# Two loads and a split moved: the first expert's second weights behind the last query and key loads, and the tail of the value split behind the second transposes, in an attention, expert and feed-forward kernel

## The chip, the cores and the metric

The kernel runs on one core of one Trainium2 chip. The metric is the device time of one execution in microseconds (us). A time without another source is that of the profiled execution of the kernel before.

## What is computed

Three layers follow one another: sigmoid attention over 4 batches of 12 heads (448 tokens, head size 64), a layer of 8 experts in which each of the 1792 tokens goes to the one with its highest logit, and a dense feed-forward layer.

```python
attn = 1.0 / (1.0 + np.exp(-(scale * q @ k.T - np.log(S))))
x = (attn @ v)                      # per head, then [1792, 768]
expert_idx = np.argmax(x @ w_gate, axis=1)
for e in range(8):                  # tokens of expert e
    h = np.maximum(xe @ w1[e], 0.0) # 768 -> 1024
    out[mask] = gate_w[mask, None] * (h @ w2[e])   # 1024 -> 768
h = x @ w_in                        # 768 -> 2048
out = (h / (1.0 + np.exp(-h))) @ w_out
```

## The kernel before, in words

Every fp32 matrix that TensorE multiplies is split into a high part (a rounded copy, fp32r) and a low part (the remainder), and a product is made of three matmuls: high by high, high by low, low by high. A split is therefore a cast and a subtraction. For weights ScalarE (ACT) does the casts (`w1h`, `w2h`) and VectorE (DVE) the subtractions (`w1l`, `w2l`); the last of the eight `w2l` of an expert is done by GpSimd (POOL).

**Attention.** The heads come in 24 pairs. `load` (lines 170 to 179) requests a pair's query `qf`, key `kf` and value `vf` on SyncE's (SP's) queue three pairs ahead. The loop at line 618 goes through two groups of keys at a time: `scores`, then `av` of the groups before; in between DVE splits the next pair's key (`split_k`) and query (`split_q`). The program's order is written out by hand, each engine works its own list in order, and so does SP with its requests. SP's requests share eight completion semaphores in turn: a request whose semaphore is still held by an unfinished transfer waits, with all requests behind it.

**The first expert.** When three of the four batches are routed, `choose` (line 360) finds the expert with most tokens and requests its weights: `w1` in six transfers of 512 KB into `stage1` (line 383) and `w2` in eight of 384 KB into `stage2` (line 385). After them stand the requests for the last pair. During the last groups `wsplit0` (line 604) splits `w1`.

**The expert tiles.** The tokens, sorted by expert, are worked in tiles of 128 rows (loop at line 791), 21 at the most. In a tile: `l1` (lines 693 to 698) gives the hidden layer in two halves; `relu`; `htrans` (line 705) transposes a half on TensorE (line 708), ACT casts it from PSUM (`hh`, line 711) and DVE subtracts (`hl`, line 712); `l2` (lines 715 to 723) takes the eight slices `w2h`/`w2l`, slices 0 to 3 with the first half and 4 to 7 with the second. In between `xtrans` transposes the next tile's rows, and `prep(t + 2)` computes which rows tile t + 2 takes: on DVE `jk` (line 531), a `SCALAR_TENSOR_TENSOR` with two inputs in SBUF, and `gi` (line 534), then on POOL the gather `gx` (line 537).

**Change of expert.** Where the tile's expert is another than the last tile's (`fr > 0`, known on ACT, DVE, SP and POOL), the new `w2` is split in two parts: slices 0 to 4 before the first `htrans` (line 807) and slices 5 to 7 (`SA` is 5) after `xtrans` (line 821). `w1` of a new expert is split at the end of the tile before (line 834): six casts and six subtractions. Each split is followed by the request for the next expert's weights into the staging tile just read. Seven tiles change the expert; they are called by their index here: 4, 5, 6, 10, 11, 13 and 16. In 4, 5 and 10 the tile after changes it as well, so that a split of `w1` ends them. The first halves' transposes of two successive tiles delimit a tile's period in what follows.

**The feed-forward layer** follows and streams its own weights.

Of the kernel before, what the change touches and what calls it, by code (L numbers as in the profile page):

```python
# [36 lines left out]
TMAX = (N + E * 127) // 128  # L37
# [20 lines left out]
def attn_moe_ffn(ctx: ExitStack, tc, qT, kT, v, wg, w1, w2, w_in, w_out, out):  # L58
    nc = tc.nc
# [67 lines left out]
    stage2 = RS.pool("stage2", 1).tile([128, FC, DM], F32, name="stage2")  # L127
# [70 lines left out]
    NG = 4  # L198
# [162 lines left out]
    def choose():  # L361
        yield 0
        pn = px_[1][:, 448:448 + E]
        nc.tensor.matmul(out=pn, lhsT=ones, rhs=run, start=True, stop=True)
        yield 0
        mx = rt.tile([128, 1], F32, tag="cmx", name="cmx")
        nc.vector.tensor_reduce(out=mx, in_=pn, axis=AX.X, op=ALU.max)
        yield 1
        cd = rt.tile([128, E], F32, tag="ccd", name="ccd")
        nc.vector.tensor_scalar(out=cd, in0=pn, scalar1=mx[:, 0:1], scalar2=-16.0, op0=ALU.is_ge, op1=ALU.mult)  # L370
        yield 1
        nc.vector.tensor_add(out=cd, in0=cd, in1=iota_e)
        yield 1
        nc.vector.tensor_reduce(out=mx, in_=cd, axis=AX.X, op=ALU.min)
        yield 1
        nc.vector.tensor_scalar(out=es, in0=mx, scalar1=16.0, scalar2=None, op0=ALU.add)
        yield 1
        nc.vector.tensor_copy(out=es_i, in_=es)
        nc.vector.tensor_scalar(out=pg_t[:, 0:1], in0=es, scalar1=float(PG), scalar2=None, op0=ALU.mult)
        yield 0  # L380
        er = reg(es_i[0:1, 0:1], (SP,), E - 1)
        for i in range(KC):
            nc.sync.dma_start(out=stage1[:, i], in_=w1[bass.ds(er, 1), :, i].rearrange("a p f -> (a p) f"))
        for f in range(FC):
            nc.sync.dma_start(out=stage2[:, f], in_=w2[bass.ds(er, 1), :, f].rearrange("a p f -> (a p) f"))
        yield 1

    def advance(x, n):
        while n > 0:
# [138 lines left out]
    def prep(t, nt=N):  # L528
        tk = keep(gs4, [128, 1], F32, "tk", t % 4)
        jk = keep(gs4, [128, NPG], F32, "jk", t % 4)  # L530
        nc.vector.scalar_tensor_tensor(out=jk, in0=iota_pg, scalar=pg_t[:, t:t + 1], in1=tt_all,
                                       op0=ALU.is_equal, op1=ALU.mult, accum_out=tk)
        gi = keep(gs4, [128, 1], I32, "gi", t % 4)
        nc.vector.tensor_scalar(out=gi, in0=tk, scalar1=-1.0, scalar2=0.0, op0=ALU.add, op1=ALU.max)
        off = bass.IndirectOffsetOnAxis(ap=gi, axis=0)
        gx = keep(gp, [128, DM], F32, "gx", t % 2)
        nc.gpsimd.indirect_dma_start(out=gx, out_offset=None, in_=Xd[0:nt], in_offset=off,
                                     bounds_check=nt - 1, oob_is_err=False)
        return gx, gi, tk
# [46 lines left out]
    def keep0():  # L586
        wi = xr_p[1].tile([128, 2, DM], F32R, tag="xr", name="wi0")
        nc.scalar.copy(out=wi[:, 0], in_=done[1])
        nc.vector.tensor_sub(out=wi[:, 1], in0=done[1], in1=wi[:, 0])
        wi0.append(wi)  # L590
# [4 lines left out]
    G = UG * len(units)  # L595
# [22 lines left out]
    for k in range(0, G + LAG, 2):  # L618
        if k < G:
            if k % NG == 0 and k // NG + 3 < G // NG:  # L620
                load(k // NG + 3)
            scores(k)
            scores(k + 1)
        xforms()
        if LAG <= k < G + LAG:
            av(k - LAG)
            av(k - LAG + 1)
        pn = k // NG + 1
        if pn < G // NG:
            if k % NG == 0:  # L630
                split_tiles(pn)
                split_k(pn)
            else:
                split_q(pn)
        if k >= LAG and (k - LAG) % NG == NG - 2:
            pr = (k - LAG) // NG
            evac(pr)
            xq += [(pr, 0), (pr, 1)]
        if k >= G - UG:
            wsplit0((k - G + UG) // 2)  # L640
        for j in (k, k + 1):
            background(j)
            if cur is None and j >= G - 8 and not tasks:
                cur = prep(0, (B - 1) * S)
                gg = gate(0, cur[1], (B - 1) * S)
            if j >= 4 * UG and j % 8 == 1 and TMIN + (j - 4 * UG) // 8 < TMAX:
                t = TMIN + (j - 4 * UG) // 8
                nc.sync.dma_start(out=Yd[t * 128:(t + 1) * 128], in_=zero)
# [56 lines left out]
    def htrans(t, half, hs):  # L705
        pt = px_[half]
        for j in range(HB // 128):
            nc.tensor.transpose(pt[:, j * 128:(j + 1) * 128], hs[:, j * 128:(j + 1) * 128], ident)
        hh = keep(hp, [128, HB], F32R, f"hh{half}", 0)
        hl = keep(hp, [128, HB], F32R, f"hl{half}", 0)  # L710
        nc.scalar.copy(out=hh, in_=pt)  # L711
        nc.vector.tensor_sub(out=hl, in0=pt, in1=hh)  # L712
        return hh, hl

    def l2(py, hh, hl, fs):
        for f in fs:
            c = slice((f % 4) * 128, (f % 4) * 128 + 128)
            for n in range(2):
                ys = slice(n * YB, n * YB + YB)
                o = py[:, n, 0:YB]  # L720
                nc.tensor.matmul(out=o, lhsT=hh[:, c], rhs=w2h[:, f, ys], start=(f == 0), stop=False)  # L721
                nc.tensor.matmul(out=o, lhsT=hh[:, c], rhs=w2l[:, f, ys], start=False, stop=False)  # L722
                nc.tensor.matmul(out=o, lhsT=hl[:, c], rhs=w2h[:, f, ys], start=False, stop=(f == FC - 1))  # L723
# [4 lines left out]
    def psy(t):  # L728
        return keep(ps_y, [128, 2, 512], F32, "y", 0)
# [24 lines left out]
    h0 = htrans(0, 0, hs0)  # L754
    hs1 = relu(0, 1, ph1)
    until(x3, "tt")
    split2(range(2, 4), (3,))
    nxt, nn = prep(1), prep(2)
    raws.append(rload(0))
    py = psy(0)  # L760
    l2(py, *h0, range(0, 2))
    h1 = htrans(0, 1, hs1)
# [31 lines left out]
    for t in range(TMAX):  # L794
        if t == TMIN - 1:
            xts = xload(0)
        if t >= TMIN:
            live = reg(tbl[0:1, 1, t:t + 1], (PE, ACT, DVE, SP, POOL), 1)
            ifs.enter_context(tc.If(live > 0))
        gx, gi, tk = cur  # L800
        if t > 0:
            gg = gate(t, gi)
            ph0, ph1 = psh(t, 0), psh(t, 1)
            l1(ph0, 0, *xhl, range(KC))
            l1(ph1, 1, *xhl, range(0, 3))
            if t > 1:
                with tc.If(fr > 0):
                    split2(range(0, SA))
                    if t + 1 < TMAX:
                        nc.sync.dma_start(out=stage2[:, 0:SA], in_=wsrc(w2, ne, 0, SA))  # L810
            if t == 3:
                early()
            h0 = htrans(t, 0, relu(t, 0, ph0))
            l1(ph1, 1, *xhl, range(3, KC))
            hs1 = relu(t, 1, ph1)
            if t + 1 < TMAX:
                xhl = xtrans(t + 1, nxt[0])
            if len(done) >= 2 and not wi0:
                keep0()
            if t > 1:  # L820
                with tc.If(fr > 0):
                    split2(range(SA, FC))
                    if t + 1 < TMAX:
                        nc.sync.dma_start(out=stage2[:, SA:], in_=wsrc(w2, ne, SA, FC))
            nn = prep(t + 2) if t + 2 < TMAX else None
            py = psy(t)
            l2(py, *h0, range(0, 2))
            h1 = htrans(t, 1, hs1)
            l2(py, *h0, range(2, 4))
            l2(py, *h1, range(4, 8))  # L830
        if 0 < t and t + 1 < TMAX:
            fr = reg(tbl[0:1, 0, t + 1:t + 2], (ACT, DVE, SP, POOL), 1)
            ne = reg(tbl[0:1, 2, t + 1:t + 2], (SP,), E - 1)
            with tc.If(fr > 0):
                for k in (0, KC // 2):
                    split1(range(k, k + KC // 2))
                    if t + 2 < TMAX:
                        nc.sync.dma_start(out=stage1[:, k:k + KC // 2], in_=wsrc(w1, ne, k, k + KC // 2))
        if t < 5:
            early()  # L840
        yout(t, py, gg, tk)
        if t == 1:
            nc.sync.dma_start(out=stage2[:, 0:SA], in_=wsrc(w2, ne1, 0, SA))
            nc.sync.dma_start(out=stage2[:, SA:], in_=wsrc(w2, ne1, SA, FC))
        cur, nxt = nxt, nn
# [112 lines left out]
    for s in range(len(steps) + FLAG):  # L958
        if s < len(steps):
            q, b, f = steps[s]  # L960
# [41 lines left out]
        else:  # L1002
            q, b, f = steps[s - FLAG]
            gh, gl, w = gs.pop(s - FLAG)
            if f == 0:
                py = [ps_y.tile([128, 512], F32, tag=f"y{i}", name=f"fy{s}_{i}") for i in range(2 * NTB)]
# [11 lines left out]
            if last:  # L1018
                for i in range(NTB):
                    m = b * NTB + i  # L1020
                    for n in range(2):
                        a, p = acc[:, m, n, :], py[2 * i + n][:, 0:YB]
# [68 lines left out]
```

## Time and profile before

| | |
|---|---|
| median of 3 runs | 1069.47 us (1064.09 to 1070.98) |
| profiled execution | 1065.88 us, of which the span is 1064.1 us |
| mean granted TensorE clock | 0.989 of full speed |

PE is TensorE's matmul stream, SPq, POOLq and so on are the engines' instruction queues. Times in rows are us from the start of the span. In a timeline row the first number is the start, the second the length of the group from first start to last end, x the number of instructions, and the bracket the idle time of the engine before it with what ended it.

### The profile page before, as it was taken

What the parts mean: (1) busy time and instruction counts of PE and PEld (TensorE: products, weight loads), DVE (VectorE), ACT (ScalarE), POOL (GpSimd) and SP (SyncE); (2) the same over time, 40 slices, a digit from 0 to 9 for tenths busy, and PEclk for the clock granted to TensorE, in tenths of its full rate; (3) what the DMA queues carried; (4) which work ended last, traced back from release to release, by engine and by line L of the source; (5) the groups of instructions that cost most, each with busy time, mean ns of one, the idle gap of its engine ahead of it and who ended that gap; (6) DMA issues with size and microseconds to landing.
All of it is one profiled execution on the core that took longest, in us unless ns stands there. A gap on an engine that the chain in (4) does not pass through costs nothing. (4 is left out here: it accounts for less than half of the span.)

```text
span 1064.1 us, 17019 instructions
## 1 busy us (share of the span) xinstructions
PE 1022.5 (96%) x6418; PEld 902.6 (85%) x6418; DVE 585.1 (55%) x1204; ACT 425.6 (40%) x712; POOL 109.0 (10%) x97
## 2 busy tenths in 40 slices
PE   8999997899999999999997999999999999999996
PEld 4555554688888988889897999999999999999996
DVE  3354564864894258443524666575576465557443
ACT  5555554423784257433423454332233222223110
POOL 1000001212131102311112100000000000000022
PEclk9999998999999999999998999999999999999998
DMA  5446677176797139471717656463464443466572
GB/s 172 148 144 148 199 203 218 56 200 238 245 351 295 46 121 352 166 267 46 282 34 247 229 228 234 149 240 139 149 239 150 179 178 119 178 212 232 197 284 115
DMA packets 50414, 203.00 MB, mean 191 GB/s; under 512 B 8400, under 2 KB 16848, under 8 KB 46352
## 3 DMA queue, kind: packets, MB, share of 16 engines
q1 hardware_dynamic: 43936, 182.51, 49.2%
q0 software_dynamic: 4528, 19.29, 5.2%
q8 instruction: 52, 0.85, 0.3%
q14 instruction: 42, 0.34, 0.1%
q10 hardware_dynamic: 1856, 0.01, 0.1%
HBM read 169.12 MB, written 32.66 MB: 190 GB/s over the span
## 5 line engine op out<-in xcount | busy, mean ns | idle before, releaser
L980 ACT ACTIVATE sg<-fh 128x256 f32<-128x256 f32 x112 | 43.0, 384 | 230.3 <-PE fh L978 227.7
L978 PE MATMUL fh<-rxh,w 128*128 128x256 f32 x462 | 130.4, 282 | 0.0
L977 PE MATMUL fh<-rxl,w 128*128 128x256 f32 x462 | 130.3, 282 | 0.0
L976 PE MATMUL fh<-rxh,w 128*128 128x256 f32 x462 | 130.1, 282 | 0.0
L1013 PE MATMUL fy<-w,gh 128*128 128x384 f32 x364 | 122.5, 337 | 0.4 <-DVE acc L1026 0.4
L1014 PE MATMUL fy<-w,gh 128*128 128x384 f32 x364 | 121.9, 335 | 0.0
L1015 PE MATMUL fy<-w,gl 128*128 128x384 f32 x364 | 121.8, 335 | 0.0
L981 DVE TENSOR_TENSOR sg<-sg,fh 128x256 f32<-128x256 f32 x112 | 47.1, 420 | 132.4 <-ACT sg L980 132.3
L217 ACT ACTIVATE a<-s,bias 128x896 f32<-128x896 f32 x96 | 82.9, 911 | 76.5 <-PE s L214 72.8
L723 PE MATMUL y<-w2h,hl 128*128 128x384 f32 x304 | 103.6, 341 | 9.8 <-DVE hl L712 5.5
L721 PE MATMUL y<-w2h,hh 128*128 128x384 f32 x304 | 105.7, 348 | 0.7 <-ACT hh L711 0.7
L722 PE MATMUL y<-w2l,hh 128*128 128x384 f32 x304 | 102.6, 338 | 0.4 <-POOL w2l L691 0.3
L696 PE MATMUL h<-w1h,xh 128*128 128x512 f32 x228 | 91.8, 403 | 0.2 <-ACT xh L678 0.2
L698 PE MATMUL h<-w1h,xl 128*128 128x512 f32 x228 | 90.2, 395 | 0.6 <-DVE xl L679 0.6
L697 PE MATMUL h<-w1l,xh 128*128 128x512 f32 x228 | 89.9, 394 | 0.0
L978 PEld LDWEIGHTS fh<-rxh,w 128*128 128x128 f32 x462 | 88.1, 191 | 0.0
L977 PEld LDWEIGHTS fh<-rxl,w 128*128 128x128 f32 x462 | 87.8, 190 | 0.0
L976 PEld LDWEIGHTS fh<-rxh,w 128*128 128x128 f32 x462 | 87.7, 190 | 0.0
L712 DVE TENSOR_TENSOR hl<-x,hh 128x512 fp32r<-128x512 f32 x38 | 26.2, 689 | 110.9 <-ACT hh L711 105.5
L230 PE MATMUL o<-a,vf 128*64 128x448 f32 x384 | 83.4, 556 | 0.0
L985 DVE TENSOR_TENSOR gl<-sg,gh 128x256 fp32r<-128x256 f32 x112 | 47.8, 426 | 52.9 <-ACT gh L984 52.9
L984 ACT CAST gh<-sg 128x256 fp32r<-128x256 f32 x112 | 45.5, 407 | 67.7 <-DVE sg L981 67.7
(218 smaller groups left out, 2172.1 us busy)
## 6 DMA issues: line engine op xcount, KB each, us to landing
rxh<-Td SPq DMA_DIRECT2D x35, 768.0 KB, 4.3
rxl<-Td SPq DMA_DIRECT2D x35, 768.0 KB, 6.0
stage<-w SPq DMA_DIRECT2D x14, 1536.0 KB, 8.1
stage<-w SPq DMA_DIRECT2D x8, 1920.0 KB, 9.7
raw<-w_in SPq DMA_DIRECT2D x13, 768.0 KB, 6.2
raw<-w_out SPq DMA_DIRECT2D x13, 768.0 KB, 6.7
stage<-w SPq DMA_DIRECT2D x8, 1152.0 KB, 7.1
Yd<-ys SPq DMA_DIRECT2D x19, 384.5 KB, 4.2
```

Source lines behind the costliest of these rows:

```text
L696: nc.tensor.matmul(out=ph, lhsT=xh[:, k], rhs=w1h[:, k, cs], start=(k == 0), stop=False)
L697: nc.tensor.matmul(out=ph, lhsT=xh[:, k], rhs=w1l[:, k, cs], start=False, stop=False)
L698: nc.tensor.matmul(out=ph, lhsT=xl[:, k], rhs=w1h[:, k, cs], start=False, stop=(k == KC - 1))
L721: nc.tensor.matmul(out=o, lhsT=hh[:, c], rhs=w2h[:, f, ys], start=(f == 0), stop=False)
L722: nc.tensor.matmul(out=o, lhsT=hh[:, c], rhs=w2l[:, f, ys], start=False, stop=False)
L723: nc.tensor.matmul(out=o, lhsT=hl[:, c], rhs=w2h[:, f, ys], start=False, stop=(f == FC - 1))
L976: nc.tensor.matmul(out=ph, lhsT=ih[:, k], rhs=xh[:, k], start=(k == 0), stop=False)
L977: nc.tensor.matmul(out=ph, lhsT=ih[:, k], rhs=xl[:, k], start=False, stop=False)
L978: nc.tensor.matmul(out=ph, lhsT=il[:, k], rhs=xh[:, k], start=False, stop=(k == KC - 1))
L1013: nc.tensor.matmul(out=o, lhsT=gh[:, c], rhs=w[1][:, 0, ys], start=(f == 0), stop=False)
L1014: nc.tensor.matmul(out=o, lhsT=gh[:, c], rhs=w[1][:, 1, ys], start=False, stop=False)
L1015: nc.tensor.matmul(out=o, lhsT=gl[:, c], rhs=w[1][:, 0, ys], start=False, stop=last)
```

## The change

The eight requests for `w2` of the first expert are taken out of `choose` and become a function of their own, `stage2load`, which the attention loop calls after the step in which the last pair's loads are requested. In the expert tiles the block with `split2(range(SA, FC))` and the request behind it are moved from behind `xtrans` to behind `htrans` of the second half; `prep(t + 2)`, the first part of `l2` and the second `htrans` now stand ahead of it.

```diff
@@ choose
         for i in range(KC):
             nc.sync.dma_start(out=stage1[:, i], in_=w1[bass.ds(er, 1), :, i].rearrange("a p f -> (a p) f"))
+        ers.append(er)
+        yield 1
+
+    ers = []
+
+    def stage2load():
         for f in range(FC):
-            nc.sync.dma_start(out=stage2[:, f], in_=w2[bass.ds(er, 1), :, f].rearrange("a p f -> (a p) f"))
-        yield 1
+            nc.sync.dma_start(out=stage2[:, f], in_=w2[bass.ds(ers[0], 1), :, f].rearrange("a p f -> (a p) f"))
@@ the attention loop
             evac(pr)
             xq += [(pr, 0), (pr, 1)]
+        if len(ers) == 1 and k >= (G // NG - 4) * NG:
+            stage2load()
+            ers.append(None)
         if k >= G - UG:
@@ a tile
             if len(done) >= 2 and not wi0:
                 keep0()
+            nn = prep(t + 2) if t + 2 < TMAX else None
+            py = psy(t)
+            l2(py, *h0, range(0, 2))
+            h1 = htrans(t, 1, hs1)
             if t > 1:
                 with tc.If(fr > 0):
                     split2(range(SA, FC))
                     if t + 1 < TMAX:
                         nc.sync.dma_start(out=stage2[:, SA:], in_=wsrc(w2, ne, SA, FC))
-            nn = prep(t + 2) if t + 2 < TMAX else None
-            py = psy(t)
-            l2(py, *h0, range(0, 2))
-            h1 = htrans(t, 1, hs1)
             l2(py, *h0, range(2, 4))
             l2(py, *h1, range(4, 8))
```

SP's queue around the last pair's loads, with the semaphores that each request waits for, before (`qf`, `kf` and `vf` are the last pair's; `stage_98` is `stage2`; DMAHW0 to DMAHW7 are the eight completion semaphores):

```order
L385 DMA stage_98<-w 128x768 [waits DMAHW4_49]
L385 ISA
L385 DMA stage_98<-w 128x768 [waits DMAHW5_49]
L176 DMA qf_1726<-qT 128x448 [waits DMAHW6_49,DVE_49]
L177 DMA kf_1725<-kT 128x512 [waits DMAHW7_49]
L178 DMA vf_1727<-v 128x512 [waits DMAHW0_49,PE_49]
```

The same place now (`stage_84` is `stage1`):

```order
L383 DMA stage_84<-w 128x1024 [waits DMAHW4_49]
L176 DMA qf_1718<-qT 128x448 [waits DMAHW5_49,DVE_49]
L177 DMA kf_1717<-kT 128x512 [waits DMAHW6_49]
L178 DMA vf_1719<-v 128x512 [waits DMAHW7_49,PE_49]
L391 ISA
L391 DMA stage_98<-w 128x768 [waits DMAHW0_49]
```

The three loads have moved ahead of all eight requests for `w2`, straight behind the six for `w1`; the value's now takes the semaphore of the first `w1` transfer.

DVE's list in a tile, from the end of `xtrans` to the split of the next `w1`, before:

```order
L679 TENSOR_TENSOR xl_2035<-t_0_2037,xh_2034 128x384
L821 COMPARE_AND_BRANCH
L691 TENSOR_TENSOR w2l<-stage_98,w2h 128x768 x2
L821 UNCONDITIONAL_BRANCH x2
L531 SCALAR_TENSOR_TENSOR jk_2211,tk_2210<-iota_pg,pg_t,tt_all 128x112
L534 TENSOR_SCALAR gi_2213<-tk_2210 128x1
L712 TENSOR_TENSOR hl_0_2247<-x_138,hh_0_2246 128x512
L95 TENSOR_LOAD tbl
L834 COMPARE_AND_BRANCH
L685 TENSOR_TENSOR w1l<-stage_84,w1h 128x1024 x6
```

and now:

```order
L687 TENSOR_TENSOR xl_2035<-t_0_2037,xh_2034 128x384
L536 SCALAR_TENSOR_TENSOR jk_2211,tk_2210<-iota_pg,pg_t,tt_all 128x112
L539 TENSOR_SCALAR gi_2213<-tk_2210 128x1
L720 TENSOR_TENSOR hl_0_2247<-x_138,hh_0_2246 128x512
L833 COMPARE_AND_BRANCH
L699 TENSOR_TENSOR w2l<-stage_98,w2h 128x768 x2
L833 UNCONDITIONAL_BRANCH x2
L95 TENSOR_LOAD tbl
L842 COMPARE_AND_BRANCH
L693 TENSOR_TENSOR w1l<-stage_84,w1h 128x1024 x6
```

`jk`, `gi` and `hl` of the second half have moved ahead of the two subtractions, which now stand straight ahead of the six of `w1`. On POOL the gather `gx` has likewise moved ahead of its subtraction.

ACT's list at the same place, before:

```order
L678 CAST xh_2034<-t_0_2037 128x384
L821 COMPARE_AND_BRANCH
L689 CAST w2h<-stage_98 128x768 x3
L821 UNCONDITIONAL_BRANCH x2
L711 CAST hh_0_2246<-x_138 128x512
L95 TENSOR_LOAD tbl
L834 COMPARE_AND_BRANCH
L684 CAST w1h<-stage_84 128x1024 x6
```

and now:

```order
L686 CAST xh_2034<-t_0_2037 128x384
L719 CAST hh_0_2246<-x_138 128x512
L833 COMPARE_AND_BRANCH
L697 CAST w2h<-stage_98 128x768 x3
L833 UNCONDITIONAL_BRANCH x2
L95 TENSOR_LOAD tbl
L842 COMPARE_AND_BRANCH
L692 CAST w1h<-stage_84 128x1024 x6
```

The cast of the second half, `hh`, has moved ahead of the three casts of `w2`, which now stand straight ahead of those of `w1`. The lines of the changed kernel lie 5 to 12 higher.

## Rows read from the trace of the kernel before

**Rows 1.** The page: busy time of TensorE, and its granted clock in 40 slices.

```profile
PE 1022.5 (96%) x6418; PEld 902.6 (85%) x6418; DVE 585.1 (55%) x1204; ACT 425.6 (40%) x712; POOL 109.0 (10%) x97
...
PEclk9999998999999999999998999999999999999998
```

**Rows 2.** Timeline of TensorE at the end of attention.

```profile
179.93 0.74 PE L214 MATMUL s<-qh,kh 64*128 64x448 f32 x2 [6.29 <-DVE qh L195]
```

**Rows 3.** Timeline of VectorE at the end of attention.

```profile
175.21 0.43 DVE L190 CAST kh<-kf 128x512 fp32r<-128x512 f32 x1 [8.97 <-DMA kf<-kT]
```

**Rows 4.** Timeline of SP's queue from 145 to 185 us.

```profile
149.69 3.29 SPq L383 DMA_DIRECT2D stage<-w  x6
153.16 9.51 SPq L385 DMA_DIRECT2D stage<-w  x8
164.28 0.34 SPq L177 DMA_DIRECT2D kf<-kT  x1
```

**Rows 5.** Line 383 by itself: issue to landing of its six transfers.

```profile
DMA to landing us min/median/max: 5.1/7.1/8.7
```

**Rows 6.** Timeline of ScalarE: the first casts of the first expert's `w2`.

```profile
193.72 1.58 ACT L689 CAST w2h<-stage 128x768 fp32r<-128x768 f32 x2
```

**Rows 7.** Two stretches: length, busy time and count of PE, PEld, DVE, ACT, POOL, PEclk, DMA, GB/s.

```profile
166.31:169.38 3.07, 3.07 (x22) 1.53 (x20) 0.00 (x0) 1.91 (x2) 0.00 (x0) 1.00 1.37 200
179.93:184.98 5.05, 5.05 (x20) 2.65 (x21) 3.48 (x4) 2.02 (x2) 2.22 (x2) 0.57 0.62 170
```

**Rows 8.** Five periods of tiles: 4, 5, 6, 7 and 10 (columns as in rows 7).

```profile
283.31:303.62 20.31, 18.81 (x100) 16.41 (x99) 20.10 (x25) 16.22 (x22) 6.49 (x3) 1.00 0.99 356
303.62:324.25 20.63, 18.80 (x99) 16.41 (x98) 20.60 (x28) 15.55 (x21) 6.82 (x3) 1.00 0.94 339
324.25:343.90 19.65, 18.57 (x99) 16.50 (x98) 7.22 (x12) 6.13 (x10) 4.02 (x3) 1.00 0.77 300
343.90:362.18 18.28, 18.28 (x99) 16.53 (x98) 3.06 (x8) 4.03 (x7) 1.99 (x2) 1.00 0.14 45
398.74:418.40 19.66, 18.57 (x99) 16.50 (x98) 17.08 (x21) 15.38 (x21) 6.01 (x3) 1.00 0.97 341
```

**Rows 9.** Timeline of TensorE: transposes in tiles 4 and 10, the stop, the next tile.

```profile
289.94 0.60 PE L708 MATMUL x<-ident,hs 128*128 128x128 f32 x4
...
404.04 0.60 PE L708 MATMUL x<-ident,hs 128*128 128x128 f32 x4
...
408.16 0.44 PE L723 MATMUL y<-w2h,hl 128*128 128x384 f32 x1 [1.08 <-DVE hl L712]
...
415.84 0.40 PE L697 MATMUL h<-w1l,xh 128*128 128x512 f32 x1
```

**Rows 10.** Timeline of VectorE: tile 4, tile 8 (`jk` alone), tile 10.

```profile
288.88 1.82 DVE L691 TENSOR_TENSOR w2l<-stage,w2h 128x768 fp32r<-128x768 f32 x2
290.62 1.93 DVE L531 SCALAR_TENSOR_TENSOR jk<-iota_pg,pg_t,tt_all 128x112 f32<-128x112 f32 x1
...
292.66 0.68 DVE L712 TENSOR_TENSOR hl<-x,hh 128x512 fp32r<-128x512 f32 x1
293.25 6.89 DVE L685 TENSOR_TENSOR w1l<-stage,w1h 128x1024 fp32r<-128x1024 f32 x6
...
367.14 0.33 DVE L531 SCALAR_TENSOR_TENSOR jk<-iota_pg,pg_t,tt_all 128x112 f32<-128x112 f32 x1
...
408.21 6.91 DVE L685 TENSOR_TENSOR w1l<-stage,w1h 128x1024 fp32r<-128x1024 f32 x6
```

**Rows 11.** Timeline of GpSimd in tile 4.

```profile
289.74 2.67 POOL L691 TENSOR_TENSOR w2l<-stage,w2h 128x768 fp32r<-128x768 f32 x1 [16.17 <-ACT w2h L689]
```

**Rows 12.** Timeline of ScalarE in tile 4.

```profile
287.32 2.34 ACT L689 CAST w2h<-stage 128x768 fp32r<-128x768 f32 x3
290.57 0.59 ACT L711 CAST hh<-x 128x512 fp32r<-128x512 f32 x1 [0.91 <-PE x L708]
291.08 5.81 ACT L684 CAST w1h<-stage 128x1024 fp32r<-128x1024 f32 x6
```

## The prediction

> **What bounds the kernel now.** I read the page first, to see which engine is short of idle time. TensorE is busy for 96% of the span, and its granted clock is a nine in nearly every slice but dips in the seventh, which is 160 to 186 us [rows 1]. So the places worth reading are the few in which TensorE stands still. I went through its timeline for idle brackets. The longest in the middle of the kernel is 6.29 us before the scores of the last pair at 179.93, put down to VectorE's split of the query [rows 2]. That split only stands behind the key's split, and this one had waited 8.97 us, from 166.24 to 175.21, for the key itself to arrive [rows 3]. SP's timeline says why: the six requests for `w1` and the eight for `w2` lie ahead of the pair's; the eight alone hold SP for 9.51 us, and the key is requested at 164.28 and lands 10.9 us later [rows 4].
>
> The stop costs more than its length. The step that follows takes 5.05 us at a mean granted clock of 0.57, that is mostly at the lower level of 1.2 GHz, where the same step of the pair before, from 166.31, took 3.07 at 2.4 GHz [rows 7]. So 1.98 us follow from the stop. Together 6.29 + 1.98 = 8.27 us.
>
> Then the tiles. An undisturbed period is 18.28 us with TensorE busy throughout; one with a change of expert is 19.65 or 19.66 (five of the seven, tiles 6 and 10 shown), and 20.31 and 20.63 in tiles 4 and 5 [rows 8]. The surplus of 1.37 in the five is one stop of 1.08 and its restart, at the third matmul on the second half's slices, which waits for `hl` [rows 9]. In tiles 4 and 5 VectorE is busy for 20.10 of 20.31 and 20.60 of 20.63 us: there VectorE is the bound, not TensorE [rows 8]. That difference decides what the second edit is worth.
>
> **The first edit: the loads.** It adds and removes no transfer; it changes SP's order. The last `w1` request is issued near 152.7 [rows 4] and `w1` lands 8.7 us later at the latest [rows 5], at about 161.4. Query and key now follow at once, and at the row's 0.34 us for an issue [rows 4] they are under way before 154. If transfers land in the order of their requests, they come right behind `w1`. They are 480 KB against the 3072 KB of `w1`, which took from 149.7 to about 161.4 [rows 4, 5], so some 1.8 us later, near 163. VectorE wants the key at 166.24 [rows 3] and the query some 6 us after that. I take the wait as gone, all of the 8.27 us. The ends: nothing is gained if the pair lands as late as now, and no more than 8.27 us can be. What is late next? The `w2` requests move behind three more transfers (736 KB, about 2 us of SP and transfer) and their semaphores now wait for query, key and value among others. If the eight again take 9.51 us from about 155 on, the last is issued near 165 and lands, with the 10.9 us of the key as the price, near 176; their first reader, ScalarE's cast, stands at 193.72 [rows 6] and would come to 185.4 when all before it is 8.27 us sooner. Nine us hide it. The price beyond that cover would be one us per us. The `w1` split that VectorE and ScalarE do beside these steps fills idle time of 8.97 us that is in the row [rows 3]; I cost it at nothing.
>
> **The second edit: the split's tail.** It removes and adds no arithmetic. Per change of expert it moves three casts, two subtractions on VectorE, one on GpSimd and a request on SP behind `hh`, `jk`, `gi`, `gx` and `hl`. I follow tile 4. `hh` starts at 290.57 with ScalarE idle before it, so it gains nothing; the next cast begins 0.51 later, at 291.08 [rows 12]. The three casts of `w2` stand there now, one each 0.74 ((2.34 - 0.86) / 2), the last from 292.56 to 293.42 [rows 12]. VectorE is through `jk` by 289.4 and idles until `hh` ends at 291.16; `hl` then ends at 291.85 instead of 293.34 [rows 10]. So the stop on `hl` is gone in every one of the seven. The gather `gx` is issued while GpSimd has nothing else to do. SP's request for the next tail waits for GpSimd as before and comes some 3 us later, with a period of over 18 us until its reader; what stands behind it on SP waits for `w1`'s subtractions anyway.
>
> What comes instead? The two subtractions run to 293.82, paced by VectorE (0.87 each start, 1.82 for both [rows 10]). GpSimd's subtraction asks at about 293.5. In the kernel before it asked at 289.74, while VectorE's two ran until 290.70, and ended at 292.41: 1.71 us after they let go [rows 10, 11]. And `jk`, begun in its turn, took 1.93 us instead of 0.33 and ended with GpSimd's [rows 10, 11]. So one waits for the other whole. Now GpSimd gets through from 293.82 to 295.53. That is 5.59 us after the start of the transposes at 289.94 [rows 9]. When does TensorE need this slice? In tile 10 the stop began at 408.16 - 1.08 = 407.08, after 14 matmuls behind the transposes, which end at 404.64: 0.174 us each [rows 9]. The slice is read by the 32nd, so without a stop at 407.08 + 16 x 0.174 = 409.86, 5.82 behind the start of the transposes. The slack is 0.2 us, and I take no stop.
>
> In tiles 6, 11, 13 and 16 nothing else follows, and the gain is 1.37 each, 5.48 in all. In tiles 4, 5 and 10 the six subtractions of `w1` come next. Their first cast starts near 293.3 and is ready near 294.4, so the first subtraction asks behind GpSimd and is held until 295.53, against 293.25 before [rows 10, 12]: 2.28 us late. Since VectorE is the bound in 4 and 5, both pass this on, 4.56 us. Afterwards TensorE has some lead over the subtractions left: in tile 10 they end at 415.12 and the last one is read at 415.84 [rows 9, 10], 0.72. So tiles 4 to 6 lose 4.56 - 0.72 = 3.84 before tile 6's gain. In tile 10 the subtractions begin at 404.04 + 5.59 = 409.63 instead of 408.21 and end at 416.54: TensorE reads 0.70 later than before, in spite of the stop it was spared.
>
> Here a rule can be set against the rows. The Trainium skill, SBUF — State Buffer, section Who interferes with whom, says that a VectorE instruction with two SBUF inputs and a GpSimd instruction that reads SBUF exclude each other for the whole instruction, and that the order of issue decides who waits. It speaks against this edit, which puts GpSimd's subtraction ahead of the six of `w1`. By that rule the edit is worth what I sum next; with a port merely shared it would be rival one. The trace agrees with it: `jk` at 1.93 against 0.33 [rows 10].
>
> **The sum.** First edit -8.27; second -5.48 + 3.84 + 0.70 = -0.94; together -9.2 us. On the profiled execution's own 1065.88 us that is 1056.7; this execution lies 3.6 us under the median of the runs, and the median less 9.2 is 1060.3. I forecast 1060. That is 0.9% less, where about 1% is what a measurement of this kernel can tell from no change. Bounds of the unknown: the second edit between -4.4 (rival one) and about +3 (a fall of the clock in the longer stops of tiles 4 to 6, at 1.98 [rows 7], and a stop of a few tenths on GpSimd's slice in seven tiles); the first between -8.27 and 0, nearest to -8.27. The forecast's own range is 1056 to 1064.
>
> **Rivals.** One: VectorE's subtractions of `w1` are not held. For it speaks that no row shows a subtraction of `w1` beside one of GpSimd; against it `jk`, which has two inputs in SBUF like them. Then the first of them runs at 294.4, 1.15 late in tiles 4 and 5, which costs 2.3 - 0.72 = 1.6, and tile 10 gains 0.5: the second edit gives -5.48 + 1.6 - 0.5 = -4.4, the sum -12.7, the time 1057. Chance 0.25.
>
> Two: the pair's loads are only half in time, because in a run the transfers share the engines and do not follow their order, or the query's split meets the `w1` split on VectorE. Half of 8.27 stays: 1064 to 1065. Against it speaks the margin of 3 us at the key. Chance 0.12.
>
> Three, the other side: GpSimd comes last. If the first cast of `w1` were ready before GpSimd asks at 293.5, VectorE would run its eight subtractions in a row, as it ran the two with GpSimd waiting, and GpSimd would wait for all. Its slice would come at 293.8 + 6.9 + 1.7 = 302.4, 12.5 us behind the transposes where TensorE wants it 5.8 behind: a stop of 6.7 in each of tiles 4, 5 and 10. With the first edit, the four gains and tile 10's old stop that is -8.27 - 5.48 - 1.37 + 20.1 = +5.0, about 1074 or, with one fall of the clock, 1076. It decides from a cast that comes 0.9 us earlier than I derive; nothing shows one. Chance 0.05.
>
> **How the numbers follow.** Forecast 0.5, rivals 0.25, 0.12 and 0.05; 0.08 is left to what I do not see, on both sides. Rival one lies under 1058.8, the bound of 1%, and so does about a third of the forecast's range: faster by over 1%: 0.40. Within 1%: 0.54, the rest of the forecast, rival two and most of three. Slower by over 1%: 0.06, the rest. The range is 1053 to 1067: it takes in rival one in a good run and rival two in a poor one, as the runs of before are 7 us apart, and leaves out rival three.
>
> **What would show it.** Right: no idle bracket before the last pair's scores, no wait on `kf`, 3.1 us for each of these steps and a nine in the seventh slice; no wait of L731 (now) on `hl` in the second half; periods of 18.3 in tiles 6, 11, 13, 16; `jk` at 0.33 in all; first `w1l` of tiles 4, 5 and 10 over 2 us long; periods of tiles 4 and 5 longer than before. Wrong: first `w1l` of 1.2 us that starts 1.1 later than before (rival one), a GpSimd subtraction of over 5 us (rival three), a wait on `kf` that remains (rival two), or a first cast of `w2` that waits for its transfer.

## The result, and the profile after

| | before | after |
|---|---|---|
| median, in the first comparison | 1069.73 us (1064.09 to 1071.29, 8 runs) | 1057.59 us (1054.31 to 1059.68, 8 runs) |
| ratio, 95% interval | | 0.9893 [0.9869, 0.9917] |
| the same two kernels again, on another chip | 1065.75 us (11 runs) | 1057.50 us (6 runs), 0.9931 [0.9908, 0.9955] |
| profiled execution | 1065.88 us | 1056.73 us, of which the span is 1055.0 us |

The two intervals meet only between 0.9908 and 0.9917; I speak of 0.9% less, and 9.15 us less by the two profiled executions. The page's clock row is the first thing to look at: [rows 1] had one dip in the seventh slice and one in the 22nd, the beginning of the feed-forward layer; neither digit dips now. In the seventh slice no fall of the clock is left; in the 22nd one of two is left, too short to change the digit.

```profile
PE 1020.8 (97%) x6418; PEld 897.2 (85%) x6418; DVE 577.5 (55%) x1204; ACT 425.7 (40%) x712; POOL 100.0 (9%) x97
...
PEclk9999999999999999999999999999999999999998
```

**The end of attention.** VectorE's timeline now shows the last pair's key and query split without a bracket ahead of them, where [rows 3] had 8.97 us:

```profile
166.44 0.42 DVE L190 CAST kh<-kf 128x512 fp32r<-128x512 f32 x1
...
172.73 0.39 DVE L195 CAST qh<-qf 128x448 fp32r<-128x448 f32 x1
```

TensorE's first scores of that pair follow the matmuls ahead of them directly, where [rows 2] had 6.29 us, and two windows show that this step (the second row) now lasts as long as the same step of the pair before it, at full clock; compare [rows 7]. Columns as there.

```profile
173.86 0.48 PE L214 MATMUL s<-qh,kh 64*128 64x448 f32 x2
```

```profile
166.60:169.67 3.07, 3.07 (x23) 1.54 (x21) 3.00 (x6) 1.91 (x2) 0.00 (x0) 1.00 0.99 199
173.86:176.94 3.08, 3.08 (x23) 1.59 (x22) 2.88 (x3) 1.90 (x2) 0.13 (x1) 1.00 1.01 389
```

The first casts of `w2`, 193.72 before [rows 6], start at 185.65 without a wait for their transfer, although the eight requests are now issued last:

```profile
185.65 1.58 ACT L697 CAST w2h<-stage 128x768 fp32r<-128x768 f32 x2
```

Matched matmul by matmul, TensorE stood 0.29 us behind the kernel before ahead of the stop and 8.07 ahead of it behind the last pair: 8.36 us gained.

**A wait that is new.** At 176.8 us VectorE comes to stand still for a store, and TensorE soon after for VectorE. SP's timeline shows why: the store of a finished unit's rows (`Xd`, line 261) is issued at 173.12, behind all eight `w2` requests and behind a zero fill (line 656) that waited for its completion semaphore until 172.69.

```profile
156.87 8.76 SPq L391 DMA_DIRECT2D stage<-w  x8
172.69 0.33 SPq L656 DMA_DIRECT2D Yd<-w  x1
173.12 14.71 SPq L261 DMA_DIRECT2D Xd<-xr  x3
```

```profile
181.91 0.42 DVE L253 COPY xr<-x 112x256 f32<-112x256 f32 x1 [5.13 <-DMA Xd<-xr]
```

What held the zero fill was none of the `w2` transfers. SP's waits name the store of the gates (`Gd`, line 358), which ScalarE's queue issued at 160.60: it takes its turn among the same eight semaphores, so these are not SP's alone. In the kernel before, the last pair's value request stood 6.1 us for that store.

```profile
160.60 0.31 ACTq L358 DMA_DIRECT2D Gd<-gs  x1
```

```profile
SPq L656 <- DMA Gd<-gs: 7.0, 1, 7.0
```

Two stops of TensorE follow from VectorE's lateness. The second comes about because VectorE's last `w1` subtraction now falls beside GpSimd's slice of tile 0 and takes 2.75 us, where those ahead of it take 1.22.

```profile
186.35 0.50 PE L706 MATMUL h<-w1h,xl 128*128 128x512 f32 x1 [0.75 <-DVE xl L687]
...
190.31 0.50 PE L705 MATMUL h<-w1l,xh 128*128 128x512 f32 x1 [0.43 <-DVE w1l L611]
```

```profile
187.50 2.75 DVE L611 TENSOR_TENSOR w1l<-stage,w1h 128x1024 fp32r<-128x1024 f32 x1
```

**Tile 0.** VectorE's subtraction of one `w2` slice takes 4.95 us here beside two of GpSimd, where the one ahead of it takes 0.95; TensorE waits for a slice of each. The kernel before had a fall of the clock in this place instead, and its period of 22.47 us has become 22.91.

```profile
204.28 0.95 DVE L699 TENSOR_TENSOR w2l<-stage,w2h 128x768 fp32r<-128x768 f32 x1
205.61 4.95 DVE L699 TENSOR_TENSOR w2l<-stage,w2h 128x768 fp32r<-128x768 f32 x1 [0.39 <-ACT w2h L697]
```

```profile
206.13 3.61 POOL L699 TENSOR_TENSOR w2l<-stage,w2h 128x768 fp32r<-128x768 f32 x2
```

```profile
208.00 0.45 PE L730 MATMUL y<-w2l,hh 128*128 128x384 f32 x1 [1.40 <-POOL w2l L699]
...
210.62 0.45 PE L730 MATMUL y<-w2l,hh 128*128 128x384 f32 x1 [1.27 <-DVE w2l L699]
```

**The tiles with a change of expert.** Periods of tiles 4, 5, 6, 10 and 11, to be laid beside [rows 8]:

```profile
277.02:298.82 21.80, 19.90 (x98) 16.07 (x99) 19.17 (x24) 16.17 (x22) 4.84 (x3) 1.00 0.96 341
298.82:321.56 22.74, 19.85 (x99) 16.09 (x99) 20.28 (x27) 15.38 (x21) 4.86 (x3) 1.00 0.84 315
321.56:339.87 18.31, 18.31 (x100) 16.54 (x99) 6.39 (x12) 6.23 (x10) 4.03 (x3) 1.00 0.85 305
...
394.76:415.07 20.31, 19.61 (x100) 16.15 (x98) 16.51 (x22) 15.39 (x21) 4.84 (x3) 1.00 0.96 344
415.07:433.35 18.28, 18.28 (x100) 16.52 (x98) 6.38 (x12) 6.24 (x10) 4.04 (x3) 1.00 0.82 307
```

Tiles 6, 11, 13 and 16 are down to an undisturbed 18.3; tiles 4, 5 and 10 have become longer. The seven sum to 137.98 us, against 139.21 before: 1.23 gained. Tile 4 shows both sides, on VectorE, GpSimd and ScalarE:

```profile
282.77 0.32 DVE L536 SCALAR_TENSOR_TENSOR jk<-iota_pg,pg_t,tt_all 128x112 f32<-128x112 f32 x1
...
285.07 0.69 DVE L720 TENSOR_TENSOR hl<-x,hh 128x512 fp32r<-128x512 f32 x1 [1.79 <-issue]
285.81 1.83 DVE L699 TENSOR_TENSOR w2l<-stage,w2h 128x768 fp32r<-128x768 f32 x2
288.23 7.88 DVE L693 TENSOR_TENSOR w1l<-stage,w1h 128x1024 fp32r<-128x1024 f32 x6 [0.59 <-ACT w1h L692]
```

```profile
287.33 2.01 POOL L699 TENSOR_TENSOR w2l<-stage,w2h 128x768 fp32r<-128x768 f32 x1 [2.30 <-ACT w2h L697]
```

```profile
287.14 5.79 ACT L692 CAST w1h<-stage 128x1024 fp32r<-128x1024 f32 x6
```

`jk` is back at 0.32 (1.93 in [rows 10]). But the six subtractions of `w1` take 7.88 instead of 6.89 us, because the first of them is begun at 288.23 beside GpSimd's and ends 2.20 later; the other five take 1.14 from one start to the next. ScalarE's casts of `w1` have moved too: they begin 10.12 us into the period, where they began 7.77 into it [rows 12]. The profiles' sum, as the lead of TensorE over the kernel before: 8.07 us behind the last pair, 6.70 at tile 0 (1.37 given back to the new wait and what follows from it), 6.29 at tile 4, 7.57 at the feed-forward layer, and 9.07 some 20 us into it, where one of the falls of the clock of before did not occur.

### The profile page after: what moved, and what is told of

It is laid out like the page before. It is cut to its first block, busy times and chain, and to the rows that moved or that the text cites. A ratio compares the mean times of both kernels' runs of the same rounds, so it can differ in the third digit from the quotient of the medians.

```text
span 1055.0 us, 17021 instructions
## 1 busy us (share of the span) xinstructions
PE 1020.8 (97%) x6418; PEld 897.2 (85%) x6418; DVE 577.5 (55%) x1204; ACT 425.7 (40%) x712; POOL 100.0 (9%) x97
```

## The experiments

Each was timed in five rounds beside the kernel before, in three batches; the medians of the kernel before were 1064.51, 1065.75 and 1066.41 us, so ratios are what to compare between batches.

**Each edit alone.** The loads alone (`e1`, the tail left where it was), and the tail alone (`e2`, the requests left in `choose`).

> The first edit alone: the last pair's loads ahead of the second weights, the tile as before. Theory (each edit acts in its own place; of the 8 us won at the end of attention some 1.7 are lost again in tile 0): 6.3 us less by the time of tile 4, tile periods as before (20.3, 20.6, five of 19.65), a ratio to the kernel before of 0.990 to 0.994. Rival (the two edits gain only together, or the second carries most): under 4 us less, a ratio above 0.996.

Measured: 1057.83 us, 0.9936 [0.9911, 0.9961]. Its trace keeps tiles 4 to 6 as they were (20.29, 20.64, 19.67 us) and has no stop before the last pair. At tile 4 it leads the kernel before by 7.8 us, where 6.3 was expected.

> The second edit alone: the tail of the value split behind the second transposes, the loads as before. Theory (GpSimd's subtraction holds the first subtraction of the next first weights): periods of 18.3 in tiles 6, 11, 13 and 16, some 20.3 in tile 10, 21.8 and 22.7 in tiles 4 and 5, so about 1.2 us less in all, a ratio of 0.997 to 1.001; first w1l of tiles 4, 5 and 10 at 2.2 us. Rival (the stops go and nothing takes their place): 7 stops, 8 to 9.6 us less, a ratio of 0.991 to 0.993.

Measured: 1066.78 us, 1.0019 [1.0000, 1.0037], just past what the theory allowed (1.001). Alone the tail gives nothing. Its windows of tiles 4 and 5 show the same loss as in the changed kernel, and in tile 5 a clock of 0.93 besides:

```profile
285.07:306.91 21.84, 19.93 (x98) 16.10 (x99) 19.19 (x24) 16.17 (x22) 4.84 (x3) 1.00 0.97 343
306.91:331.07 24.16, 21.32 (x100) 17.62 (x99) 20.25 (x27) 15.37 (x21) 4.85 (x3) 0.93 0.78 294
```

**The changed kernel again**, beside the kernels of the second batch.

> The changed kernel itself, unaltered, beside the others on this chip. From the first edit alone (0.9936 of the kernel before) and the second alone (1.0019) the product would be 0.9955; the profiles' own account, in which the second edit gives 1.2 us where the first has gone before it and takes some 2 where it has not, would be 0.990 to 0.993. Theory: 0.989 to 0.993, so that the second edit's worth is small beside the first and not of a fixed sign. Rival: 0.995 or more, the second edit costs time with the first as it does alone.

Measured: 0.9931 [0.9908, 0.9955], at the upper edge of what the theory allowed and below the rival's. Against the loads alone (0.9936) the timing shows no worth of the second edit; its 1.2 us are read from the periods, which repeat: 21.84, 22.73, 18.30 and 20.30 us in tiles 4, 5, 6 and 10.

**Who holds the first subtraction of `w1`?** In `e4` the moved slice's subtraction goes from GpSimd to VectorE.

```diff
-                    split2(range(SA, FC))
+                    split2(range(SA, FC), ())
```

> The changed kernel with the last slice of the moved tail subtracted on VectorE, not on GpSimd. Theory (the hold by GpSimd is the price in tiles 4, 5 and 10): first w1l at 1.2 us and ended 0.8 to 0.9 us sooner than in the changed kernel in each of the three, 2 to 3 us less in all; tiles 6, 11, 13 and 16 stay at 18.3. Rival (the price is VectorE's idle time before hl, and the hold is beside it): VectorE has 0.87 us more to do in each, the time is the same or up to 2 us more.

Measured: 1055.06 us, 0.9910 [0.9889, 0.9930]. With GpSimd out, VectorE's rows in tile 4 are

```profile
285.11 2.70 DVE L699 TENSOR_TENSOR w2l<-stage,w2h 128x768 fp32r<-128x768 f32 x3
287.73 6.89 DVE L693 TENSOR_TENSOR w1l<-stage,w1h 128x1024 fp32r<-128x1024 f32 x6
```

so the six are back at 6.89: GpSimd's subtraction held the first, and rival one (not held) falls. Tile 5 shrinks to 21.22 and tile 10 to 19.52, but tile 4 stays at 21.73, above the 20.31 of before. VectorE is through its six some 0.8 us sooner there; now TensorE waits for ScalarE, whose `hs` stands behind the casts that begin 10.12 us into the period in this trace as well:

```profile
297.41 0.59 ACT L710 ACTIVATE hs<-h 128x512 f32<-128x512 f32 x1
```

```profile
298.05 0.66 PE L716 MATMUL x<-ident,hs 128*128 128x128 f32 x4 [0.56 <-ACT hs L710]
```

So tiles 4, 5 and 10, which lose 4.25 us in the changed kernel, still lose 1.87 without GpSimd: the hold is somewhat more than half of the price, and the rest comes with the tail's place. The seven periods sum to 135.60 us; the ratios, 0.9910 against 0.9893 and 0.9931 of the changed kernel, do not tell the two kernels apart.

**What made the stop of 1.08 us?** In the changed kernel two things moved ahead of the tail: `hh`/`hl`, and `prep` with `jk`. Two kernels move `prep` alone, one with the loads of the change (`e3`), one with nothing else (`e8`):

```diff
+            nn = prep(t + 2) if t + 2 < TMAX else None
             if t > 1:
                 with tc.If(fr > 0):
                     split2(range(SA, FC))
...
-            nn = prep(t + 2) if t + 2 < TMAX else None
```

> The first edit with another second one: only the preparation of tile t+2 (jk, gi, gx) goes ahead of the split's tail; the split stays ahead of the second transposes. Theory (the stop on hl came from jk, which waited for GpSimd's subtraction; with jk ahead nothing on VectorE waits for GpSimd but a first subtraction that comes later anyway): jk 0.33 us in all tiles, no stop on hl in the second half, first w1l started 0.3 us sooner than in the kernel before; periods of 18.3 in tiles 6, 11, 13, 16, up to 18.6 in tile 10, 20.0 and 20.3 in tiles 4 and 5; 5 to 7 us less than the changed kernel, a ratio to the kernel before of 0.982 to 0.986. Rival (hl came late because the casts and subtractions of the second weights stood ahead of it): stops of 0.3 to 1.1 us on hl remain, and it is no faster than the changed kernel.

Measured: 1048.88 us, 0.9858 [0.9834, 0.9881], within the theory's range.

> The kernel before with one thing moved: the rows' computation for the tile after next (jk, gi and the gather) ahead of the split's tail. Loads and tail stay where they were. Theory (the stop of 1.08 us in every tile with a change of expert came from jk alone, held 1.9 us by GpSimd's subtraction): jk 0.33 us in all seven, no stop at hl of the second half, the seven periods 131 to 133 us in sum where the kernel before has 139.2, and 6.5 to 8 us less in all: 0.992 to 0.994. Rival (the stop came from the tail's casts and subtractions standing ahead of hl): periods as before but for some tenths, 0.998 to 1.000.

Measured: 1058.87 us, 0.9928 [0.9906, 0.9950], as the theory had it, and the seven periods sum to 131.63 us, 7.58 less than before. Its windows of tiles 4, 5, 6, 10 and 11, and VectorE in tile 4:

```profile
285.75:305.32 19.57, 18.55 (x99) 16.47 (x98) 19.02 (x24) 16.22 (x22) 4.82 (x3) 1.00 1.00 364
305.32:325.74 20.42, 18.53 (x99) 16.45 (x98) 20.00 (x27) 15.44 (x21) 4.90 (x3) 1.00 0.94 358
325.74:344.02 18.28, 18.28 (x99) 16.52 (x98) 6.12 (x12) 6.14 (x10) 4.08 (x3) 1.00 0.85 312
398.86:417.38 18.52, 18.52 (x99) 16.45 (x98) 16.02 (x21) 15.28 (x21) 4.83 (x3) 1.00 0.99 365
417.38:435.66 18.28, 18.28 (x99) 16.53 (x98) 6.30 (x12) 6.13 (x10) 4.02 (x3) 1.00 0.81 305
```

```profile
291.26 0.33 DVE L531 SCALAR_TENSOR_TENSOR jk<-iota_pg,pg_t,tt_all 128x112 f32<-128x112 f32 x1
...
291.84 1.83 DVE L691 TENSOR_TENSOR w2l<-stage,w2h 128x768 fp32r<-128x768 f32 x2
293.59 0.69 DVE L712 TENSOR_TENSOR hl<-x,hh 128x512 fp32r<-128x512 f32 x1
```

The tail's two subtractions stand ahead of `hl` as in the kernel before, and the stop is gone all the same. So it came from where `prep` stood, and the row in it that changed is `jk`, 0.33 us instead of 1.93; the tail did not have to move, and moving it is what lengthens tiles 4, 5 and 10. (`gi` and, on GpSimd, the gather `gx` move with `jk`; no kernel moves `jk` by itself.) With the tail in its old place the first `w1l` of tile 4 starts at 283.02 in the trace of `e3`, 8.8 us into the period instead of 11.2. It is held there too, for 2.09 us.

**The new wait on the store.** The last two of the eight requests are put one step later, so that the zero fill and the store are issued ahead of them: with nothing else (`e5`), and together with `prep` ahead (`e6`). `stage2load` takes the slices as its argument there.

```diff
         if len(ers) == 1 and k >= (G // NG - 4) * NG:
-            stage2load()
+            stage2load(range(0, 6))
+            ers.append(None)
+        elif len(ers) == 2:
+            stage2load(range(6, FC))
             ers.append(None)
```

> Changed kernel, with the last two of the eight requests for the first expert's second weights put one step of the attention loop later, so that the store of a finished unit's rows is issued ahead of them and of the zero fill that waits for a semaphore. Theory (the new wait of VectorE on that store, 3.7 to 5.1 us at 180 to 182 us in four profiles, comes from the queue in front of the store): the wait goes or shrinks below 1.5 us, TensorE's stops of 0.4 to 1.3 us at 184 to 190 us go, and the time is 1.0 to 1.7 us under the changed kernel's. Rival one (the store lands late because the weights' transfers are under way beside it, wherever it stands): the wait stays above 3 us and the time within 0.5 us. Rival two (the wait goes but tile 0's subtractions on GpSimd bind anyway): no wait on the store, TensorE stands longer at 206 to 212 us instead, time within 0.5 us.

Measured: 1055.39 us, 0.9908 [0.9884, 0.9932]. The store is issued at 165.65, 7.47 us sooner than in the changed kernel, and the bracket names it no longer:

```profile
164.00 0.33 SPq L659 DMA_DIRECT2D Yd<-w  x1
165.65 0.33 SPq L261 DMA_DIRECT2D Xd<-xr  x1
172.44 1.12 SPq L391 DMA_DIRECT2D stage<-w  x2
```

```profile
178.90 0.42 DVE L253 COPY xr<-x 112x256 f32<-112x256 f32 x1 [2.35 <-PE x L251]
```

That the wait came from the queue is shown: the gates' store now holds the seventh `w2` request, until 172.44, and nothing that VectorE waits for. In the traces the wait's price up to tile 0 follows its length. TensorE's lead over the kernel before, behind the last pair less that at tile 0, is 1.37 us where VectorE waited 5.13 (the changed kernel), 0.71 at 4.61 (its second trace), 0.45 at 4.36 (`e3`), 0.37 at 4.28 (`e4`), nothing at 3.73 (`e1`), and nothing in `e5` and `e6`, without the wait. In time it is not shown: 2.1 us under the changed kernel of the same batch, with overlapping intervals, and tile 0 behind it varies by more than that from trace to trace.

> Changed kernel with the rows' computation for the tile after next ahead of the moved tail, the tail itself back ahead of the second half's transposes (0.9858 of the kernel before, when run by itself), and with the two late requests as in the kernel beside it. Theory: the two gains add, 1.0 to 1.7 us under the former, 0.984 to 0.985. Rival: 0.9858 as before, tile 0 binds.

Measured: 1048.82 us, 0.9848 [0.9823, 0.9874]; against 0.9858 no difference that can be measured.

**Tile 0, again.** Slices 5 and 7 go from GpSimd to VectorE, on top of `e6` (`e7`).

```diff
-    split2(range(4, FC), (5, 7))
+    split2(range(4, FC), ())
```

> The kernel beside it (both rearrangements) with the two subtractions of the first expert's second weights that GpSimd does in tile 0 between 204 and 208 us, slices 5 and 7, done by VectorE. Theory (VectorE's subtraction there takes 4.9 us because GpSimd's two hold it, and TensorE's stops of 1.4 and 1.3 us behind it come from that): no VectorE subtraction over 1.3 us there, both stops gone, 2.0 to 2.7 us less than the kernel beside it. Rival (VectorE, with two more subtractions, is the bound in tile 0 anyway): the stops are as long in sum, time within 0.5 us.

Measured: 1047.11 us, 0.9832 [0.9807, 0.9857], and in the third batch

> The kernel of the last comparison with slices 5 and 7 of tile 0 on VectorE, unaltered, as the reference for the kernel beside it. Theory: 0.982 to 0.985 of the kernel before. Rival (part of its gain was the profiled execution's clock): 0.986.

1047.91 us, 0.9831 [0.9810, 0.9853]. VectorE does four slices in less time than it needed for one while GpSimd held it, and TensorE's stops of 1.4 and 1.3 us are gone: tile 0's period is 19.95 and 19.97 us in the two traces, where it is 22.5 to 25.3 in those of the kernel before, the changed one and the seven others up to here.

```profile
202.25 3.55 DVE L702 TENSOR_TENSOR w2l<-stage,w2h 128x768 fp32r<-128x768 f32 x4
```

Against `e3`, whose tile 0 has the 4.9 us and both stops at full clock, that is 2.9 us; `e6`'s trace, 2.8 us longer in this tile, had neither, but a fall of the clock. In time it is 1.7 us against `e6`, with overlapping intervals. The ratio is the lowest of the study, shared with the next kernel and not told apart from `e6`.

**GpSimd out of every tile behind the first.** The same for the last slice of each change of expert, on top of that (`e9`).

> The kernel beside it with the last slice's subtraction of every change of expert on VectorE too, so that GpSimd subtracts nothing in tiles 1 and later. Theory (a subtraction on GpSimd holds VectorE about as long, 0.9 to 1.0 us, as VectorE's own would take, 0.95): first w1l 1.2 us long, but begun as much later; no difference beyond 0.8 us. Rival (GpSimd's subtraction costs more than VectorE's own, as in the changed kernel, where the same edit gave some 2 us): 1.5 to 3 us less.

Measured: 1048.60 us, 0.9831 [0.9812, 0.9851], level with the kernel beside it. The periods tell more than the time: tile 5 shrinks from 20.45 to 20.11, but the five tiles 6, 10, 11, 13 and 16 grow by 0.4 to 0.7 each, for a new stop at `hl`, which stands behind VectorE's added slice. In tile 10 the six of `w1` follow, and the first of them is held for 2.29 us with GpSimd's slice; even there the slice costs less on GpSimd.

## Why the prediction was right, and where it was not

1060.0 was forecast and 1057.6 measured, within the range; the first comparison's 1.07% lies just past the 1% that had the greatest chance, the second's 0.69% within it.

- **The first edit at its place: right.** Forecast 8.27, measured 8.36, by the steps named: no wait for the key, the step at full clock, the `w2` transfers in time. The loads alone carry it (`e1`).
- **The term that was mis-sized: 8.27 was carried to the end at full size, with the `w1` split beside the last pair "at nothing".** I asked of the moved requests only when their own data are read. What stands behind them on SP is late too: the store of `Xd`, and with it VectorE, which splits `w1` there. SP is held there by the gates' store, of another queue that shares the eight semaphores; the prediction has no term for it. That gave back 1.37 us in the first trace and 0.71 in the second (8.83 us ahead, then 8.12 at tile 0), but nothing in the loads' own kernel (8.55 at both places), where VectorE waited 3.73 us. The loads alone measured 6.8 us less with an interval of 4.1 to 9.5 in which 8.27 lies, so that time alone does not decide this term; the traces do.
- **The second edit in sum: right.** Forecast 0.94 less, the periods show 1.23: tiles 4 to 6 lose 2.26 (forecast 2.47), tile 10 loses 0.65 (0.70), and 11, 13 and 16 gain 4.12 (4.11). GpSimd's subtraction ends 5.52 us behind the start of the transposes, 5.59 being forecast, and holds the first `w1l`, which ends 2.26 us later in tile 4's period than before (2.28). Rival one (not held) and rival three (GpSimd last) did not happen. But the hold is not the whole price: without it tile 4 is nearly as long (`e4`), because ScalarE's list binds there too, and the prediction follows that list no further than the first cast of `w1`. In time the sum is too small to show: 0.9936 without the second edit, 0.9893 and 0.9931 with it.
- **What the prediction had in hand and did not use:** it named `jk`'s 1.93 us as the hold, and credited the move of `hh` and the tail with the end of the stop. Moving `prep` with `jk` was enough.
- **Not foreseen:** 1.5 us in the feed-forward layer, where the profiles' 9.15 us meet the forecast's 9.2 only because this stands against the 1.37. It is a matter of the clock in one execution: in the second trace the lead is 7.87 us at the start of that stretch and 7.79 behind it.

The hold is the place where the rows met a rule. The row of the six subtractions shows 7.88 us beside GpSimd and 6.89 without it. The Trainium skill, SBUF — State Buffer, section Who interferes with whom, says that a VectorE instruction with two inputs in SBUF and a GpSimd instruction that reads SBUF exclude each other for the whole instruction; the traces agree (2.20 against 1.22 us for the first `w1l`, 1.93 against 0.33 for `jk`).

## What to carry to other kernels

Before a block of work is moved, find the one instruction in it, or behind it, that is long for its size, and move that one: here a `jk` of 0.33 us that took 1.93 explained the whole stop, and with the loads moved in both, moving `prep` with it gave 0.9858 where moving the block gave 0.9893 and 0.9931. A subtraction handed to GpSimd holds the instructions of VectorE with two inputs in SBUF that come beside it; what that costs depends on whom TensorE waits for in that tile (taking it from GpSimd won 0.34 us in tile 5 and cost 0.4 to 0.7 in five others). And when requests are moved in a queue, list everything that now stands behind them, stores and zero fills too, and whatever else takes their semaphores, on other queues as well.

## What the runs showed that was not expected

- **One order, two outcomes of the hold.** In tile 0 VectorE's subtraction beside GpSimd's two takes 4.9 us in eight traces (the changed kernel twice, `e1` to `e5`, `e8`) and 2.00 us, with 1.98 for the instruction behind it, in two (the kernel before and `e6`). Those two had a fall of the clock earlier in the tile, and GpSimd's first subtraction began 0.7 us ahead of VectorE's there. In the eight VectorE's began 0.5 us ahead of GpSimd's first, while GpSimd's gather was still under way, and still ended behind the second. The gather by itself does not hold: in the two, a subtraction of VectorE that began beside it took 0.96 us. The same section of the Trainium skill adds that the order of issue decides who waits; these rows do not show it. What decides is open.
- **The same stop, with and without a fall of the clock.** TensorE's stops of 1.4 and 1.3 us in tile 0 came with 6.8 us at 1.2 GHz, begun behind the first stop or in the second, in three traces (the changed kernel's second, `e1` and `e5`), and with no fall in the changed kernel's first, `e2` to `e4` and `e8`. The stop of 2.14 to 2.17 us in tile 5 was followed by one in `e2` and `e5`, and by none in both of the changed kernel. Tile 5 lasts 24.2 and 24.3 us with it and 22.7 without, so that such a fall costs 1.5 us. Single traces of one kernel differ by that much, which is why no verdict here rests on the spans of single traces.
